# Inversions' transfers on GpSimd's queue, tokens of the first sixteen units listed within the recurrence, those of the last eight counted unit by unit

## The chip, the core and the metric

The kernel runs on one core of one Trainium2 chip. The core has five engines that work side by side, each through its own queue in program order: TensorE (PE, with its weight loads shown as PEld), VectorE (DVE), ScalarE (ACT), GpSimd (POOL) and SyncE (SP), which here only issues transfers. Transfers are issued by SP, ACT or POOL and carried by 16 DMA engines. The metric is the device time of one execution in microseconds (us).

## The reference

An attention-like recurrence over 768 steps (4 batches, 8 heads, head size 40), and behind it a mixture of 8 experts in which each expert keeps only the 80 tokens with the highest gates:

```python
for t in range(S):                       # recurrence, per batch and head
    y[:, :, t] = einsum('bhd,bhde->bhe', r[t], state)
    Sa = einsum('bhde,bhe->bhd', state, a[t])
    state = state * w[t] - outer(Sa, b[t]) + outer(v[t], k[t])
...
x = y as rows, (3072, 320)               # one row per token
logits = x @ w_gate                      # 8 experts
expert_idx = argmax(logits, axis=1)
gate_w = softmax(logits)[expert_idx]
for e in range(8):
    tok_idx = tokens with expert_idx == e
    keep = the 80 of them with the highest gate_w
    out[keep] = gate_w * (relu(x[keep] @ w1[e]) @ w2[e])   # 320 -> 1024 -> 320
```

All other rows of the output are zero.

## The kernel before

The 3072 tokens are cut into 24 units of 128 tokens: 12 chunks of 64 steps times 2 pairs of batches. A unit n goes through `prepare(n)` (decays, scaled keys, the score matrices `nt` and `psi`), waits until the unit triangular matrices of its set are inverted, goes through `solve(n)` (off-diagonal blocks of the inverse) and `finish(n)` (the step of the state: W, UL, the sum into `st`, the decay of `st`, the rows y through `xT` into `xg`, the logits into `lgp`). Units of the same pair depend on each other through `st`, so the 24 finishes are a chain in two strands. Rings of ten buffers (`LOOK = 10`) let prepare run at most ten units ahead of finish, and `nt` has room for three sets.

`invert(j)` inverts the 32x32 blocks of a set of units: sets 0 and 1 have two units, sets 2 to 6 have four (units 4-7, ..., 20-23). Its blocks go to DRAM and come back laid out one block per partition (`out_go`, then `fetch`), 30 elimination steps run on GpSimd (tiles `lt` and `tmp`), the result goes to DRAM (`put`) and comes back into `nt` and `d1` (`back_go` and `low_go`). For sets 2 to 6, `fetch` and `put` are issued by GpSimd, one transfer each of 128 pieces of 4 KB; `out_go` (4 transfers), `back_go` (2) and `low_go` (4) are issued by SP, of 1024, 1024 and 512 pieces of 128 bytes each. `lt` is a single buffer, so a fetch also waits for the put of the set before.

`gate(gi)` turns the logits of four units into gates; every second group (eight units) a ranking of ten rounds (`rank`) on VectorE merges the top 80 of each expert into `cand`.

All this is recorded as operations with engine, estimated cost and dependencies in `Plan`, and `Plan.order()` writes them out as one fixed order per engine: at each step it takes the operation that can start earliest, and among those the one with the lowest `when`, which is half the due time less the length of the chain behind the operation. An engine works through its order strictly; an operation whose input is late holds up all behind it on that engine.

After the last unit a second part runs, engine by engine in plain order: the rest of the ranking, the merge of the eight lists into a threshold per expert (lines 900 to 926), the choice of tokens over all 24 units by comparing gates with the threshold, counting positions and building one-hot matrices (lines 931 to 966), the indices (968 to 974), eight gathers of 80 rows from `x_rows` in DRAM (L991), and then the experts one after the other: transposes of the rows (L1001, L1003), first layer (L1016), second layer (L1035, L1039), output (L1047 to L1051). Expert weights, 2.6 MB each, are loaded by SP as soon as the recurrence's buffers are free (L885, L887).

## Time and profile before

| | us |
|---|---|
| median of 3 runs | 545.68 (545.13 to 548.99) |
| profiled execution, own time | 545.97 |
| its span, first to last instruction | 544.3 |
| outside the span | 1.67 |
| PE / PEld / DVE / ACT / POOL busy | 395.5 / 349.8 / 311.9 / 170.8 / 247.9 |

A row of a timeline is: start, length, engine, line of the program, operation, result <- operands, count; in brackets how long the engine had been idle before it and what ended the idle time. "SPq" and "ACTq" are the queues of transfers, and their lengths are the time that issuing took, not the time to landing. Busy shares are averages over very different stages: up to about 420 us the recurrence runs, from there to 470 us the choice of tokens, and then the experts.

### The profile page before, as it was taken

To read this page: it belongs to the slowest core of one execution; us is meant where nothing else is said; L and a number is where in the kernel's file an instruction comes from. 1 tells how busy PE (TensorE), PEld (TensorE's weight loads), DVE (VectorE), ACT (ScalarE), POOL (GpSimd) and SP (SyncE) were. 2 spreads that over 40 slices of the span, in tenths; PEclk is the share of its full clock that TensorE was granted. 3 is DMA by queue.
4 is the path that set the end of the run, shared out by engine and by line. 5 is a ranking of instruction groups with operands and counts; after the bars stand their busy time and mean duration, and the time that the engine had idled before them with its cause. 6 is when DMAs were issued, how large, how long until landed. Compare 5 with 4: busy or idle time off the path is not lost. (4 is left out here: it accounts for less than half of the span.)

```text
span 544.3 us, 25618 instructions
## 1 busy us (share of the span) xinstructions
PE 395.5 (73%) x11383; PEld 349.8 (64%) x11383; DVE 311.9 (57%) x643; ACT 170.8 (31%) x339; POOL 247.9 (46%) x459
## 2 busy tenths in 40 slices
PE   1834577889958998888888696988795005478995
PEld 1734466778847887777777585878684004377895
DVE  6849956675636675873688543667434785012111
ACT  1521252435523634444534242434251000011100
POOL 7000883699569838982689405882000000501012
PEclk9975797789979997999999589899799555599999
DMA  9668577656595577578766345446400799994000
GB/s 118 99 129 143 85 125 122 128 83 96 118 167 113 95 164 99 107 156 144 122 125 135 88 75 127 95 95 112 88 16 4 218 336 352 297 337 127 17 19 24
DMA packets 233922, 69.39 MB, mean 127 GB/s; under 512 B 214100, under 2 KB 228692, under 8 KB 233812
## 3 DMA queue, kind: packets, MB, share of 16 engines
q1 hardware_dynamic: 200948, 55.76, 50.1%
q10 hardware_dynamic: 30656, 5.12, 5.9%
q0 software_dynamic: 2208, 6.89, 3.9%
q8 instruction: 89, 1.46, 1.1%
q14 instruction: 21, 0.17, 0.1%
HBM read 52.74 MB, written 14.99 MB: 124 GB/s over the span
## 5 line engine op out<-in xcount | busy, mean ns | idle before, releaser
L558 POOL TENSOR_TENSOR tmp<-lt 128x30 f32<-128x30 f32 (+9 forms) x150 | 86.6, 577 | 30.9 <-DMA lt<-blocks 19.5
L560 POOL TENSOR_TENSOR lt<-lt,tmp 128x30 f32<-128x30 f32 (+9 forms) x150 | 89.8, 599 | 11.8
L740 DVE TENSOR_TENSOR UL<-ps,mask 128x832 f32<-128x832 f32 x24 | 24.5, 1022 | 53.7 <-PE ps L735 35.1
L480 PE MATMUL ps<-ah,kbT 40*64 40x64 f32 x1536 | 33.3, 231 | 14.9 <-ACT kbT L471 6.3
L394 PE MATMUL ps<-ident,kb 128*128 128x128 f32 x192 | 33.7, 331 | 10.6 <-ACT lgp L793 4.8
L480 PEld LDWEIGHTS ps<-ah,kbT 40*64 40x64 f32 x1536 | 28.7, 143 | 18.9 <-ACT kbT L471 7.6
L424 DVE TENSOR_TENSOR_SCAN P<-dec,begins 128x520 f32<-128x520 f32 x24 | 31.8, 1324 | 12.4 <-ACT dec L415 12.1
L471 ACT COPY kbT<-ps 128x1024 f32<-128x1024 f32 x24 | 24.3, 1013 | 38.4 <-PE ps L394 30.5
L394 PEld LDWEIGHTS ps<-ident,kb 128*128 128x128 f32 x192 | 27.0, 171 | 14.4 <-ACT lgp L793 5.4
L1051 POOL DMA_INDIRECT out_dram<-y,idx_s x8 | 7.3, 918 | 60.9 <-DVE y L1050 60.9
L1022 DVE TENSOR_SCALAR hT<-hp 128x320 f32<-128x320 f32 x8 | 3.9, 492 | 50.2 <-ACT hT L1024 50.2
L432 DVE TENSOR_TENSOR_SCAN iv<-dec,ends 128x512 f32<-128x512 f32 x24 | 30.5, 1271 | 1.8
L765 DVE TENSOR_TENSOR st<-ps,st 128x832 f32<-128x832 f32 (+1 forms) x24 | 23.9, 994 | 10.0 <-PE ps L754 9.6
L455 DVE TENSOR_TENSOR kb<-rawkb,ps 128x320 f32<-128x320 f32 x48 | 22.4, 479 | 12.4 <-ACT st L711 3.1
L394 PE MATMUL ps<-ident,rawa 128*128 128x128 f32 x96 | 16.7, 302 | 16.9 <-DMA rawa<-in_a_dram 16.9
L1016 PE MATMUL hp<-xe,w 128*64 128x80 f32 x512 | 28.1, 239 | 1.2 <-DVE xe L1005 1.2
L651 ACT COPY rv<-ps 128x1024 f32<-128x1024 f32 x24 | 24.3, 1014 | 12.8 <-PE ps L394 11.2
L695 PE MATMUL ps<-VL,psi 64*64 64x104 f32 x768 | 25.5, 269 | 3.3 <-issue 3.1
L603 DVE STREAM_TRANSPOSE d<-nt 128x256 f32<-128x256 f32 x24 | 10.2, 431 | 30.5 <-DMA nt<-solved 15.9
L735 PE MATMUL ps<-W,nt 64*64 64x104 f32 x768 | 25.5, 273 | 3.1 <-ACT nt L629 1.3
L833 POOL TENSOR_TENSOR ids<-gsm,tok 128x32 f32<-128x32 f32 x6 | 3.2, 531 | 51.4 <-DVE gsm L825 51.3
L415 ACT COPY dec<-ps 128x512 f32<-128x512 f32 x24 | 14.1, 588 | 39.1 <-PE ps L394 30.8
(173 smaller groups left out, 997.1 us busy)
## 6 DMA issues: line engine op xcount, KB each, us to landing
w<-in_moe_w_dram SPq DMA_DIRECT2D x8, 1280.0 KB
w<-in_moe_w_dram SPq DMA_DIRECT2D x8, 1024.0 KB
x_rows<-xg SPq DMA_DIRECT2D x24, 160.5 KB
rawkb<-in_k_dram SPq DMA_DIRECT2D x48, 80.0 KB
rawkb<-in_b_dram SPq DMA_DIRECT2D x48, 80.0 KB
raww<-in_w_dram SPq DMA_DIRECT2D x48, 80.0 KB
rawr<-in_r_dram ACTq DMA_DIRECT2D x96, 40.0 KB
VL<-in_v_dram SPq DMA_DIRECT2D x96, 40.0 KB
```

The lines of the kernel that those rows point to most:

```text
L394: nc.tensor.matmul(o, lhsT=i, rhs=ident, is_transpose=True, **mat)
L424: nc.vector.tensor_tensor_scan(at("P", n), at("dec", n)[:, 0 : H * SEG], begins, 0.0, op0=Alu.mult, op1=Alu.add)
L432: nc.vector.tensor_tensor_scan(at("iv", n)[:, ::-1], at("dec2", n)[:, ::-1], at("ends", n)[:, ::-1], 0.0, op0=Alu.mult, op1=Alu.add)
L471: nc.scalar.copy(at("kbT", n).rearrange("p (k c) -> p k c", k=2), ps[:, bank(kk) : bank(kk) + 2, :])
L480: nc.tensor.matmul(ps[half(to(q, bb)), b0 + q, T * i : T * i + T], lhsT=at("kbT", n)[half(q, D), s0 : s0 + T], rhs=chain(at("ah", n), half ...
L558: e.tensor_tensor(out=tv, in0=m3[:, 0:k_, s : s + 1].to_broadcast([128, k_, n_]), in1=row(s)[:, s + 1 :].unsqueeze(1).to_broadcast([128, k ...
L560: e.tensor_tensor(out=m3[:, 0:k_, s + 1 :], in0=m3[:, 0:k_, s + 1 :], in1=tv, op=Alu.add)
L651: nc.scalar.copy(at("rv", n).rearrange("p (k c) -> p k c", k=2), ps[:, bank(kr) : bank(kr) + 2, :])
L695: nc.tensor.matmul(ps[half(q ^ bb), b0 + q, X * i : X * i + X], lhsT=at("psi", n)[half(bb), 256 * q + T * i : 256 * q + T * i + T], rhs=at ...
L735: nc.tensor.matmul(ps[half(bb), b0 + q, X * i : X * i + X], lhsT=nt[half(x), q, i, :], rhs=at("W", n)[half(x), o : o + X], **mat)
L740: nc.vector.tensor_tensor(out=view(at("UL", n), 0, (M4 * X, 2), (1, M4 * X)), in0=view(ps[:, bank(ku), :], 0, (512, 2), (1, M4 * X)), in1= ...
L1016: nc.tensor.matmul(o[64 * g : 64 * g + 64], lhsT=w[:, 128 * f + 64 * g : 128 * f + 64 * g + 64], rhs=xe[:, c + j * (c == 2), :], start=c = ...
```

## The change

Four things are changed together.

1. For sets 3 to 6 `out_go` is issued by GpSimd, behind the end of the inversion before (the key `("fin", j - 1)`); for sets 2 to 6 `back_go` and `low_go` are issued by GpSimd too.
2. Units 0 to 15 (`NA = 16`): once their gates are known, `choose()` does the merge, the threshold, the choice, the indices (`idx_g`) and eight gathers as operations of the plan, among the work of units 16 to 23. Gates are also split into three bf16 pieces (`parts_`) so that the chosen gates can be picked by bf16 products with the same one-hot matrices. What each chosen token's rank among the 80 is, is worked out as well (`rk_a`).
3. Units 16 to 23 (`NC = 8`) are gated in smaller groups (four, two, one, one), and `count(n)` counts for each token of unit n how many of units 16 to n have the same expert and a higher gate, and adds to the earlier units' counts. `last_count()` then places the tokens of units 16 to 23 among the 80 of units 0 to 15, and a second round of eight gathers overwrites the rows that lose their place. The choice over all 24 units after the recurrence is gone.
4. Smaller moves: for units 20 to 23 the mask of `VL` is done by an ACT copy and a GpSimd product in place of one VectorE product; for units 20 to 22 the product into `xT` goes to GpSimd; `rawr` of units 20 to 23 is loaded by SP. The weights of experts 0 to 6 have buffers, expert 7 takes those of expert 0. A transfer of one element of expert 0's rows stands in SP's queue after the loads of expert 0, so the later weights are issued only when these rows have landed.

```diff
+    NA = 2 * GU * (NM // GU // 3)
+    NC = NM - NA
+    groups = [list(range(n, n + GU)) for n in range(0, NM - GU, GU)] + [[NM - 4, NM - 3], [NM - 2], [NM - 1]]
...
+            by_pool = {"out": 2 < j and not last, "fetch": 1 < j and not last, "put": 1 < j, "back": 1 < j and not late}
+
+            def move(what, n_, lag, fn, reads, writes, after=0.0, to=()):
+                on = by_pool[what]
+                add("POOL" if on else "SP", (0.6 if on else 0.75) * n_, lag, z, fn, reads, writes, None, to, after if on else 0.0)
...
-            add("SP", 3.8, 2.6, z, out_go, [("nt", n) for n in ns], [("blk", j)])
+            move("out", 4, 2.6, out_go, [*(("nt", n) for n in ns), ("fin", j - 1 if by_pool["out"] else -1)], [("blk", j)])
...
-                    nc.sync.dma_start(nt[T * x : T * x + C, :, 0:C], solved[j][x, 0].rearrange("q h (s t) -> s (q h) t", s=C))
-            add("SP", 1.9, 3.0, z + 5, back_go, [("sol", j)], [("nt", n) for n in ns])
+                    queue("back").dma_start(nt[T * x : T * x + C, :, 0:C], solved[j][x, 0].rearrange("q h (s t) -> s (q h) t", s=C))
+            move("back", 2, 3.0, back_go, [("sol", j)], [("nt", n) for n in ns], BACK)
...
-            add("DVE", 0.7, 0.2, z - 1, lv_mask, [klv, ("consts", 0)], [("VL", n)])
+            if n < NM - GU:
+                add("DVE", 0.7, 0.2, z - 1, lv_mask, [klv, ("consts", 0)], [("VL", n)])
+            else:
+                add("ACT", 0.62, 0.2, z - 1, lv_copy, [klv], [("VL", n)])
+                add("POOL", 1.2, 0.2, z - 0.9, lv_keep, [("consts", 0)], [("VL", n)])
...
+        def choose():
+            for i in range(rounds):
+                put("DVE", 1.1 if i < rounds - 1 else 0.5, 0.1, z, best_go, [kM], [kM, kT])
+            put("DVE", 0.7, 0.1, z, sel_go, [kT, *[("gates", g) for g in range(NA // GU)]], [kS])
...
+            for e in range(E):
+                put("POOL", 1.2, 2.5, z + e * 0.01, lambda e=e: nc.gpsimd.indirect_dma_start(
+                    out=rows[e], out_offset=None, in_=x_dram[0][:, :],
+                    in_offset=bass.IndirectOffsetOnAxis(ap=idx_g[:, e : e + 1], axis=0)), [("idx", 0), ("xd", False)], [("row", e)], None, over_rows[e])
...
+            put("POOL", 1.4, 0.1, z, lambda: g_.tensor_tensor(out=gt_, in0=gt_, in1=eq_, op=Alu.add), [kEQ], [kGT])
+            def rank_go():
+                v_.tensor_reduce(rk_a, gt_, axis=AX, op=Alu.add)
+                v_.tensor_scalar_add(rk_a, rk_a, 0.5)
...
+        def count(n, oh):
+            put("DVE", 0.2 + 0.06 * k_, 0.1, z, lambda: v_.tensor_scalar(less[:, 0:nb], o_b[:, 0:nb], gw, None, op0=Alu.is_lt),
+                [("bb", j) for j in range(nb // 128)] + [("gw", g_)], [kLT])
+            put("DVE", 0.35 + 0.13 * k_, 0.1, z, lambda: v_.tensor_tensor_reduce(
+                out=more[:, 0:nk], in0=less[:, 0:nk], in1=all_s(), scale=1.0, scalar=0.0, op0=Alu.mult, op1=Alu.add, accum_out=lt_c[:, kc]),
+                [ks_, kLT], [kMO, ("ltc", k_)])
...
+        def last_count():
+            put("DVE", 0.75, 0.1, z, idx_go, [kid], [("idx", 1)])
+            put("POOL", 8.0, 2.5, z, rows_c, [("idx", 1), ("xd", True)], [("row", e) for e in range(E)])
...
-        for i, op in enumerate((Alu.is_gt, Alu.is_equal)):
-            nc.vector.tensor_tensor(out=sel[:, :, i, :], in0=gates.rearrange("p m e -> p e m"),
-                                    in1=tb.to_broadcast([128, E, NM]), op=op)
...
+        if e == 0:
+            nc.sync.dma_start(sink[:, 0:1], rows[0][0:1, 0:1])
...
+        if e == 1:
+            load_expert(E - 1, *weights[0])
```

How the written order moves, at three places. GpSimd, between the inversion of units 16 to 19 and that of units 20 to 23, before (`solved<-lt` is the put, `lt<-blocks` the fetch):

```order
L577 DMA solved<-lt_138 128x1024
L833 TENSOR_TENSOR ids<-gsm_154,tok 128x32
L536 DMA lt_138<-blocks 128x1024
L558 TENSOR_TENSOR tmp<-lt_138 128x30
L560 TENSOR_TENSOR lt_138<-lt_138,tmp 128x30
```

The same place on GpSimd now (L563 is `out_go` of the next set, L620 `back_go` and L627 `low_go` of the set just inverted, L569 the fetch; L973, L974, L1002 and L1003 fill constants of the counting):

```order
L610 DMA solved<-lt_136 128x1024
L893 TENSOR_TENSOR ids<-gsm_152,tok 128x4x8 x3
L563 DMA blocks<-nt_155 32x32x32 x4
L973 MEMSET rawkb_86 128x128
L974 AFFINE_SELECT rawkb_86<-rawkb_86 128x128
L620 DMA nt_154<-solved 32x32x32 x2
L569 DMA lt_136<-blocks 128x1024
L1002 MEMSET psi_123 128x256
L1003 MEMSET psi_123 128x8
L627 DMA d_0_156<-solved 32x16x32 x4
```

Ten transfers have come between the put and the next inversion's first step, and `back_go` stands behind `out_go` of the next set.

SP, at the same place, before:

```order
L377 DMA VL_131<-in_v_dram 64x4x40 x4
L530 DMA blocks<-nt_157 32x32x32 x4
L587 DMA nt_156<-solved 32x32x32 x2
L594 DMA d_0_158<-solved 32x16x32 x4
L871 DMA out_dram<-zero 384x1x320
L377 DMA VL_132<-in_v_dram 64x4x40 x4
```

SP there now:

```order
L387 DMA rawkb_86<-in_b_dram 64x8x40 x2
L390 DMA VL_129<-in_v_dram 64x4x40 x4
L1252 DMA out_dram<-zero 1536x1x80
L390 DMA VL_130<-in_v_dram 64x4x40 x4
L390 DMA VL_128<-in_v_dram 64x4x40 x4
```

The ten transfers of the inversion have left SP's queue; the loads of inputs follow each other.

VectorE, from the mask of UL of unit 22 to that of unit 23, before:

```order
L740 TENSOR_TENSOR UL_133<-ps,mask 128x832
L671 TENSOR_TENSOR VL_132<-ps,mask 128x2x4x64
L765 TENSOR_TENSOR st_0_144<-ps,st_0_144 128x4x2x64
L775 TENSOR_TENSOR xT_146<-st_0_144,P_92 128x512
L740 TENSOR_TENSOR UL_133<-ps,mask 128x832
```

Now 36 instructions stand between these two masks; the last of them, the mask of unit 23 (L783) and what follows it up to the sum into `st` (L808) (L1167 and L1175 are products with a running sum, of two instructions each):

```order
L1167 ISA dec_79,counts<-ends_133,ps 128x640
L1167 ISA counts 128x1
L1158 SCALAR_TENSOR_TENSOR rawkb_86<-ps,gw_c,rawkb_86 128x128
L1175 ISA rawkb_86,counts<-rawkb_86,ps 128x128
L1175 ISA counts 128x1
L1178 SCALAR_TENSOR_TENSOR counts<-counts 128x1
L783 TENSOR_TENSOR UL_131<-ps,mask 128x832
L1182 TENSOR_TENSOR counts<-counts,ps 128x4
L1161 TENSOR_SCALAR ends_133<-kbT_134,gw_c 128x768
L1158 SCALAR_TENSOR_TENSOR rawkb_86<-ps,gw_c,rawkb_86 128x128
L808 TENSOR_TENSOR st_0_143<-ps,st_0_143 128x4x2x64
```

Counting of units 20 to 22 and the choice over units 0 to 15 stand ahead of the state's own instructions.

## Rows read from the trace of the kernel before

**Rows 1.** Windows by stage: length, busy time of each engine (instructions), granted clock, DMA share, GB/s.
```profile
300.00:350.00 50.00, 40.19 (x1252) 36.25 (x1252) 23.20 (x63) 17.16 (x34) 22.95 (x48) 0.76 0.46 94
350.00:400.00 50.00, 41.79 (x1509) 37.98 (x1513) 31.14 (x74) 18.82 (x37) 18.75 (x34) 0.93 0.46 90
400.00:421.00 21.00, 15.37 (x639) 13.22 (x628) 8.12 (x12) 7.36 (x17) 0.00 (x0) 0.97 0.04 8
421.00:470.00 49.00, 9.63 (x62) 8.11 (x63) 30.44 (x99) 0.23 (x1) 6.15 (x10) 0.50 0.96 299
434.00:462.00 28.00, 9.16 (x60) 7.90 (x60) 19.06 (x51) 0.00 (x0) 0.00 (x0) 0.50 1.06 347
470.00:537.00 67.00, 59.33 (x1444) 55.86 (x1446) 11.14 (x23) 7.16 (x23) 8.50 (x10) 0.97 0.44 129
```

**Rows 2.** Timeline from the last unit's rows to the first expert's transposes.
```profile
418.55 0.69 DVE L775 TENSOR_TENSOR xT<-st,P 128x512 f32<-128x512 f32 x1
...
420.59 0.21 ACT L793 COPY lgp<-ps 128x64 f32<-128x64 f32 x1
...
421.48 0.19 DVE L818 TENSOR_REDUCE gsm<-lg 128x4 f32<-128x32 f32 x1
...
433.72 0.35 DVE L857 MATCH_REPLACE8 cand<-cand,cand 64x208 f32<-64x208 f32 x1
...
463.22 1.02 POOL L991 DMA_INDIRECT rows<-x_rows,idx_g  x1 [0.52 <-DMA w<-in_moe_w_dram]
...
469.94 0.50 PE L1001 MATMUL xp<-ident,rows 80*128 80x80 f32 x2 [8.51 <-DMA rows<-x_rows,idx_g]
```

**Rows 3.** Timeline of GpSimd: puts, fetches and a first step of inversions.
```profile
142.57 0.61 POOL L577 DMA_DIRECT2D solved<-lt  x1 [0.31 <-DMA rawr<-in_r_dram]
148.35 0.54 POOL L536 DMA_DIRECT2D lt<-blocks  x1 [5.17 <-DMA solved<-lt]
...
247.71 0.59 POOL L577 DMA_DIRECT2D solved<-lt  x1 [0.30 <-POOL lt L549]
258.79 0.58 POOL L536 DMA_DIRECT2D lt<-blocks  x1 [10.23 <-DMA rawkb<-in_k_dram]
...
306.63 0.59 POOL L577 DMA_DIRECT2D solved<-lt  x1 [0.30 <-POOL lt L549]
326.74 0.58 POOL L536 DMA_DIRECT2D lt<-blocks  x1 [19.25 <-DMA nt<-solved]
331.41 0.23 POOL L558 TENSOR_TENSOR tmp<-lt 128x30 f32<-128x30 f32 x1 [4.09 <-DMA lt<-blocks]
...
369.54 0.59 POOL L577 DMA_DIRECT2D solved<-lt  x1 [0.30 <-POOL lt L549]
```

**Rows 4.** Timeline of SP's queue: the inversions' transfers around these puts.
```profile
266.46 1.55 SPq L587 DMA_DIRECT2D nt<-solved  x2
...
318.63 4.52 SPq L530 DMA_DIRECT2D blocks<-nt  x4
323.25 1.58 SPq L587 DMA_DIRECT2D nt<-solved  x2
...
377.26 1.16 SPq L587 DMA_DIRECT2D nt<-solved  x2
```

**Rows 5.** Source line of `out_go`: issue times, ns least/median/most, first and last start.
```profile
L530 SPq DMA_DIRECT2D blocks<-nt x28: 302/569/2438, 25.1 to 320.7; - x28
```

**Rows 6.** Source line of the puts (L577): issue to landing, all five.
```profile
DMA to landing us min/median/max: 3.0/3.9/5.5
```

**Rows 7.** Timeline of VectorE: masks of UL in the last units.
```profile
390.66 1.02 DVE L740 TENSOR_TENSOR UL<-ps,mask 128x832 f32<-128x832 f32 x1 [1.07 <-PE ps L735]
...
408.33 1.02 DVE L740 TENSOR_TENSOR UL<-ps,mask 128x832 f32<-128x832 f32 x1 [4.68 <-PE ps L735]
...
415.91 1.02 DVE L740 TENSOR_TENSOR UL<-ps,mask 128x832 f32<-128x832 f32 x1 [4.32 <-PE ps L735]
```

**Rows 8.** Groups by line and form on GpSimd: busy us, mean ns | idle before.
```profile
L558 POOL TENSOR_TENSOR tmp<-lt 128x240 f32<-128x240 f32 x10 | 8.7, 869 | 0.8
```

More of the change, by code (lines that the diff above doesn't have):

```diff
@@ L131 @@
 SLACK = 0.15
+MARGIN = 0.0
+BACK = 20.0
 USE_TAIL = True
+AFTER, CHOICE = 20.0, 10.0
 ALPHA = 0.5
+LATE_R = 4
 LOAD_R, LOAD_V = "ACT", "SP"
@@ L561, in invert @@
                 us = 2 * (0.16 + k_ * n_ / 960) if eng == "DVE" else 2 * (0.185 + 0.00195 * k_ * n_)
-                add(eng, us, 0.1, z + s * 0.1, step, own, [own[-1], tk])
+                add(eng, us, 0.1, z + s * 0.1, step, own, [own[-1], *tks])
             def end():
@@ L572, in end @@
                 diagonal(1.0)
-            add("POOL", 1.45, 0.1, z + 4, end, (), own[-1:])
+            add("POOL", 1.45, 0.1, z + 4, end, (), [own[-1], ("fin", j)])
             def put():
                 if not apart:
-                    nc.gpsimd.dma_start(solved[j].rearrange("x c q h (s t) -> (x c q h) s t", t=C), m3)
+                    queue("put").dma_start(solved[j].rearrange("x c q h (s t) -> (x c q h) s t", t=C), m3)
                     return
@@ L580, in put @@
                 for r in range(2):
-                    nc.sync.dma_start(by[r], m3[half(r)])
-            add("SP" if apart else "POOL", 1.3 if apart else 1.0, 2.8 if apart else 4.0, z + 4.2, put, own[-1:], [("sol", j)])
+                    queue("put").dma_start(by[r], m3[half(r)])
+            move("put", 2 if apart else 1, 2.8 if apart else 4.0, put, own[-1:], [("sol", j)])
             def back_go():
@@ L858, in gate, with left, put @@
                 add("DVE", 0.82 if gs else 0.65, 0.1, z + 2 + 0.3 * i, rank, [("cd", gs)], [("cd", gs), ("cd", gs + 1)])
+        def left(name, m, o, n_, rows_=128, dtype=F32):
+            t = at(name, m)[0:rows_, o : o + n_]
+            return (t if dtype is F32 else t.bitcast(dtype)), ("left", name, m, o)
+        def put(eng, us, lag, when, fn, reads=(), writes=(), psum=None, to=()):
+            add(eng, us, lag, when, fn, reads, writes, psum, [k_[1:3] for k_ in [*reads, *writes] if k_[0] == "left"] + list(to), soft[0])
@@ new lines @@
+        o_b, kO = left("kbT", NM, 0, NC * 128)
+        ohf = [left("raww", NM + i, 0, 512, E) for i in range(2)]
+        ohb, kB = left("rawa", NM, 0, NC * 64, E, BF16)
+        rv_, kRV = left("rawa", NM + 1, 0, 2 * cap, E)
+        gwb = [left("rawa", NM + 1, 160 + 128 * i, 128) for i in range(2)]
+        pick, kPK = left("iv", NM, 0, NC * cap // 2, 128, BF16)
+        hot_c, kHC = left("dec2", NM, 0, NC * cap // 2, 128, BF16)
+        less, kLT = left("ends", NM, 0, 64 * NC, 128, BF16)
+        more, kMO = left("dec", NM, 0, 64 * NC, 128, BF16)
@@ L1055 @@
     ctx.enter_context(tc.manual_schedule())
-    for e in range(E):
-        gather(e)
     turn_x(0)
```

631 lines of the change are left out of this document (419 added, 212 removed).

## The prediction

> **What bounds the kernel now.** Read first the table by stage [rows 1]. Up to 421 us the recurrence runs with PE busy four fifths of the time and no engine full; from 421 to 470 PE is busy for 9.6 of 49 us at a granted clock of 0.50 and nothing else does matrix work; from 470 on the experts run, PE busy 59.3 of 67. The second view is the timeline across that gap [rows 2]: the last unit's product into `xT` ends at 418.55 + 0.69 = 419.24, the ranking of the last eight units at 434.1, then come the merge, the choice and the indices, the first gather is issued at 463.22, and expert 0's rows reach PE at 469.94. So 50.7 us lie between the last unit and the experts, one step waiting for the other. From there to the end of the span are 544.3 - 469.94 = 74.4 us, and 1.67 lie outside it: 419.24 + 50.7 + 74.4 + 1.67 = 545.97, the profiled execution's own time; the median, 545.68, is within 0.3 of it.
>
> The third view is the recurrence's own pace. From a put to the next set's fetch GpSimd took 5.8, 11.1 and 20.1 us (148.35 - 142.57, 258.79 - 247.71, 326.74 - 306.63) [rows 3], and a fetch is followed by the first step 4.7 us later (331.41 - 326.74). The return of the inverted blocks, `back_go`, was issued by SP 18.8, 16.6 and 7.7 us after the put (266.46, 323.25 and 377.26 against 247.71, 306.63 and 369.54) [rows 3, 4], though a put lands within 3.0 to 5.5 us [rows 6]. Inversions and the units that wait for them set the pace.
>
> **The change part by part.** *The choice leaves the gap.* What must follow the last `xT` now, in GpSimd's and VectorE's written order: three comparisons of 320 columns and a running-sum product of 768 columns stand ahead of the logits. With 0.69 us for 512 columns [rows 2] and 1.02 for 832 [rows 7] that is 1.5 + 1.0; the logits themselves are there after 420.59 + 0.21 - 419.24 = 1.6 [rows 2]. Some ten small operations of the gate at 0.19 [rows 2] and a 0.02 gap each give 2.1, so 4.6 so far. Then VectorE's sum for the ranks waits for GpSimd: six gathers at about 1.2 (1.02 and a gap) [rows 2] begin some 6.6 before the end of `xT`, and behind them two products of 640 columns, 2.3 each from 0.87 for 240 [rows 8]: -6.6 + 7.2 + 4.6 = 5.2, and with the sum itself 6.4. From there the counting of units 22 and 23 is VectorE's alone: two comparisons of 896 columns (1.8), products of 896 and 1024 (1.2 and 1.35, with the second instruction that each has), eight picks (1.6), one-hots (0.9) and a dozen small ones (2.6) make 9.5; PE's products 0.5; four index operations 0.8; the first gather 1.1 with its wait; landing 3.0, the least of the puts [rows 6], since the later weights wait behind it. The sum is 21.3, I take 21.5 for 50.7: **-29.2**. No trace shows the running-sum product or the comparison: below, they could take half (4 less), above, half again with a landing of 6.7 as in 463.22 to 469.94 (6 more).
>
> *What the moved work costs where it goes.* The choice took 19.1 us of VectorE within 434 to 462 [rows 1]; for 16 units and with the ranks it is about 20, the counting of eight units some 15, and 9 of ranking go. VectorE has room: busy 23.2 and 31.1 of 50 us, then 8.1 of 21 [rows 1]. The room is not where the orders put it, though. Between the masks of units 20 and 22 I add up 17.7 of VectorE's work against 408.33 - 390.66 = 17.7 now [rows 7], so it fits only without a wait; I add 2. Between those of units 22 and 23 stand 36 instructions: the sum into `st` 0.7, position sums 2.4, two one-hots 1.6, two running-sum products 1.7, the gate of unit 22 1.7, the small ones 3.9, with the mask 13.0 against 415.91 - 408.33 = 7.6 [rows 7], so 5.3 more. Behind the mask of unit 23 come 1.2 more before its `xT`. That is **+8.5** on 28.6 (419.24 - 390.66); bounds 0 (waits for PE now idle VectorE as long [rows 7]) and +14 (each of the two strands also waits for the GpSimd products that replace VectorE's). ACT's added copies are hidden: it is busy 18.8 of 50 and 7.4 of 21 [rows 1]; without that cover five passes per unit at 0.21 [rows 2] and more would cost 1 to 3. The loads of `rawr` that SP takes over and the finer writes of zeros cost nothing as long as SP, without four transfers that took it 4.5 us [rows 4] and six more per set, keeps ahead; if it doesn't, a unit waits some 3 for its `rawr`.
>
> *The inversions' transfers.* SP loses ten transfers per set, GpSimd gains them: four behind the put, two before the fetch, four before the first step. The nearest rows: the same 1024-piece transfers on SP's queue take 0.57 in the median [rows 5], GpSimd's own of 128 pieces 0.54 to 0.61 [rows 3]. They agree, so I take 0.6 to 0.8; below, 0.3 (SP's least); above, 4.6 (0.58 times 1024/128), if GpSimd pays by the piece. At 0.8 a put is followed by the first step after 0.6 + 3.2 + 1.6 + 0.6 + 4.7 = 10.7 (the last four are covered by the fetch's landing), against 5.8 + 4.7 = 10.5 where nothing else held it: no loss there. The return is issued about 6 after its put: 13 earlier than now for units 12 to 15, 10 earlier for 16 to 19. What that brings runs through a loop: unit 23's preparation needs unit 13's finish (`LOOK`), so the last `out_go` (318.63 [rows 4]) and its inversion come earlier by what unit 13 does. The return of the last set stays some 11 after its put, for a `VL` product of unit 20 stands ahead of it. I put unit 20's mask at 380 for 390.66: **-10.7**. Bounds: 0, since `back_go` stands behind `out_go` on GpSimd and waits with it wherever `nt` is late; and -20, if both long gaps shrink to the short one (5.3 and 14.3).
>
> *Experts.* Weights 1 to 7 now load while PE computes, at the rate of the gap (347 GB/s, 2.6 MB in 7.6 us [rows 1]), about PE's own pace; the cover of weights loaded ahead is gone. **+1.0** for PE's stalls under load; bounds 0 and +6.
>
> The sum: 545.97 - 29.2 - 10.7 + 8.5 + 1.0 = 515.6 us, 5.5% less.
>
> [...]
>
> **The rivals.** *Slower: GpSimd pays by the piece.* If one 1024-piece transfer takes c, put to first step is 0.6 + 6c + 0.6 + the larger of 4.7 and 2c. Against today's 10.5, a like one, 15.8 and 24.8 [rows 3], c = 2.3 gives 19.7 and so 9 + 9 + 4 - 5 for the four inversions that have one before them, and 4c - 6 = 3 for the last return, 20 in place of -10.7: 546, no gain left. That is the point from which it decides, four times the rows' 0.58. At 4.6 it is 38 each time, 90 more, with 12 for the last return 102, near 629. For it: the pieces are eight times those of any GpSimd transfer in the trace. Against: the same pieces cost SP no more than others.
>
> *The return stays behind `out_go`.* The change moves the transfers and nothing comes earlier, because GpSimd waits for `nt` exactly where SP did: 323.25 was issued right behind 318.63 [rows 4]. Then 526.3.
>
> *VectorE becomes the bound of the last units.* Recurrence gain 0 and the upper end of the second term, +14: 531.8. For it: the added rows stand ahead of the state's own; against: 4.3 to 4.7 us of idle time before the last masks [rows 7].
>
> *The loop gives all it can.* -20 and +3 for VectorE: 500.8.
>
> **How the numbers follow.** Forecast, 508 to 522: 0.50; return behind `out_go`: 0.15; VectorE bound: 0.15; all of the loop: 0.10; by the piece: 0.10. The range runs from 498, a little below the best case, to 537, above VectorE's case with c up to about 2; it leaves out nearly all of the slower case and some of the edges, 0.18. A measurement of this kernel tells about 1% from no change. All cases but the slower one lie more than 1% below; of that one a small part falls within 1%: faster 0.87, same 0.03, slower 0.10.
>
> **What would show it.** In the changed kernel's trace: the time from the last `xT` to expert 0's transposes near 21 (right) or above 27; GpSimd's 1024-piece transfers under 1 us each, or over 2; `back_go` issued some 6 us after its put, or later with `out_go` ahead of it; unit 20's mask near 380; some 13 us between the last two masks with VectorE busy; the experts' stretch near 75. It is wrong if these transfers are dear, if a written order makes a strand of units wait for a count, or if the weights of expert 0 come late because SP's queue holds them back.

## The result and the profile after

The changed kernel takes 551.54 us in the median of 15 executions (547.74 to 556.27), the kernel before 544.52 beside it: the ratio is 1.0139 (95% interval 1.0108 to 1.017), 1.4% slower where 5.5% faster was forecast. Ratios here leave out executions that lie more than 1.5% above the fastest of their kernel, so they differ from a quotient of the medians, and in the two series of six executions below they rest on three and on two. The profiled execution took 547.74 us, the shortest of the fifteen, with a span of 545.9, so 1.84 lie outside it.

The windows by stage of the changed kernel (columns as in [rows 1]), from the mask of UL of unit 20 to the end of the last `xT`, from there to expert 0's transposes, and from there to the end:

```profile
387.00:434.70 47.70, 37.92 (x1051) 30.48 (x1051) 32.09 (x104) 21.25 (x71) 14.18 (x20) 0.83 0.19 46
434.70:456.10 21.40, 10.85 (x83) 7.66 (x81) 14.65 (x58) 7.14 (x24) 7.83 (x12) 0.50 0.59 191
456.10:545.90 89.80, 68.19 (x1472) 62.91 (x1472) 11.77 (x24) 7.49 (x24) 13.07 (x14) 0.90 0.68 207
```

The gap of 50.7 us is indeed 21.4 now. What it gave was taken back on both sides: the stretch from unit 20's mask to the last `xT` is 47.7 for 28.6, and the experts take 89.75 for 74.4 although TensorE does the same 1472 matmuls there. Set against the forecast's terms:

| term | forecast | measured | missed by |
|---|---|---|---|
| gap, last `xT` to expert 0's transposes | -29.2 | 21.4 - 50.7 = -29.3 | 0 |
| unit 20's mask (390.66 before) | -10.7 | 387.00: -3.7 | +7.0 |
| unit 20's mask to the last `xT` | +8.5 | 47.7 - 28.6 = +19.1 | +10.6 |
| experts' stretch | +1.0 | 89.75 - 74.4 = +15.4 | +14.4 |
| sum, from 545.97 | 515.6 | 547.7 (0.2 more outside the span) | +32 |

These are single executions. In nine profiled executions with all of the inversions' transfers on GpSimd's queue (this one and those of the experiments) unit 20's mask stands at 387.0 to 399.4, at 390.0 in the median, so the -3.7 of this row is the favourable end of that spread: the gain of the second term is nearer to nothing.

The timeline of the gap, changed kernel, for comparison with [rows 2]:

```profile
434.03 0.68 DVE L818 TENSOR_TENSOR xT<-st,P 128x512 f32<-128x512 f32 x1
...
438.73 0.80 DVE L1113 TENSOR_REDUCE small_a<-kb 80x8 f32<-80x640 f32 x1
...
453.06 0.16 DVE L1218 SCALAR_TENSOR_TENSOR idx_c<-small_a 80x8 int32<-80x8 f32 x1
...
453.49 1.00 POOL L1223 DMA_INDIRECT nt<-x_rows,idx_c  x1 [11.94 <-DVE small_a L1231]
...
456.15 0.50 PE L1295 MATMUL xp<-ident,nt 80*128 80x80 f32 x2 [3.59 <-DMA nt<-x_rows,idx_c]
```

The ranks' sum ends 4.8 us after `xT`, the indices are there at 453.2, and expert 0's rows reach TensorE 2.7 us after the first gather's issue began: the parts differ from the forecast's by a few us (6.4; 9.5 of counting, here 12.3), the sum does not.

GpSimd's transfers, to be read beside [rows 3, 5]. The source line of `out_go` in the changed kernel (ns least, median, most) with the time from the start of an issue to its landing, in us:

```profile
L563 POOL DMA_DIRECT2D blocks<-nt x16: 783/784/840, 145.6 to 320.6; - x16
DMA to landing us min/median/max: 4.8/5.4/6.0
```

GpSimd's timeline of the changed kernel around two puts (L610 the put, L563 `out_go`, L620 `back_go`, L569 the fetch):

```profile
144.95 0.61 POOL L610 DMA_DIRECT2D solved<-lt  x1 [0.31 <-POOL lt L582]
145.56 3.17 POOL L563 DMA_DIRECT2D blocks<-nt  x4
148.72 1.56 POOL L620 DMA_DIRECT2D nt<-solved  x2
154.21 0.57 POOL L569 DMA_DIRECT2D lt<-blocks  x1 [3.93 <-DMA x_rows<-xg]
...
259.63 0.61 POOL L610 DMA_DIRECT2D solved<-lt  x1 [0.30 <-POOL lt L582]
260.24 3.13 POOL L563 DMA_DIRECT2D blocks<-nt  x4
263.38 1.24 POOL L893 TENSOR_TENSOR ids<-gsm,tok 128x32 bf16<-128x32 f32 x3
265.56 1.58 POOL L620 DMA_DIRECT2D nt<-solved  x2 [0.94 <-DMA solved<-lt]
268.87 0.58 POOL L569 DMA_DIRECT2D lt<-blocks  x1 [1.73 <-DMA blocks<-nt]
```

A transfer of 1024 pieces takes GpSimd 0.78 us in the median of 16, 0.84 at most, one of 128 pieces 0.57 to 0.61 in these rows: it does not pay by the piece. `back_go` is issued 3.8 and 5.9 us after these puts (about 6 was forecast). But from put to fetch it now takes 9.3, 10.1, 9.2 and 9.6 us, where before it took 5.8, 5.4 (199.89 - 194.50), 11.1 and 20.1 (148.35 - 142.57 and so on, [rows 3]): the long waits shrank, the short ones grew. The last put is at 369.84, before at 369.54.

VectorE's masks of UL of units 20, 22 and 23 in the changed kernel's timeline, for [rows 7]:

```profile
387.00 1.02 DVE L783 TENSOR_TENSOR UL<-ps,mask 128x832 f32<-128x832 f32 x1 [0.68 <-PE ps L778]
...
409.70 1.02 DVE L783 TENSOR_TENSOR UL<-ps,mask 128x832 f32<-128x832 f32 x1 [0.93 <-ACT sT L729]
430.68 1.02 DVE L783 TENSOR_TENSOR UL<-ps,mask 128x832 f32<-128x832 f32 x1 [5.45 <-remote]
```

TensorE's timeline ahead of the last of these masks (L749, L762 and L778 are unit 23's steps towards it, L797 its product of keys with VL; rows of the choice and the counting in between):

```profile
416.26 0.68 PE L830 MATMUL ps<-wsel,xT 40*64 40x48 f32 x32 [1.18 <-ACT raww L1142]
417.60 0.69 PE L749 MATMUL ps<-rv,sT 40*64 40x64 f32 x32 [0.65 <-ACT xg L841]
...
420.53 1.67 PE L762 MATMUL ps<-st,ah 40*64 40x104 f32 x32
422.13 0.71 PE L1155 MATMUL ps<-rawa 8*128 8x512 bf16 x2
422.77 0.47 PE L1148 MATMUL ps<-ident,rawa 128*128 128x128 f32 x1
...
423.39 1.67 PE L778 MATMUL ps<-W,nt 64*64 64x104 f32 x32
424.83 0.69 PE L797 MATMUL ps<-VL,kb 64*64 64x64 f32 x12
426.31 0.47 PE L797 MATMUL ps<-VL,kb 64*64 64x64 f32 x2 [0.79 <-issue]
...
429.17 0.48 PE L797 MATMUL ps<-VL,kb 64*64 64x64 f32 x4 [0.95 <-issue]
430.58 0.54 PE L797 MATMUL ps<-VL,kb 64*64 64x64 f32 x9 [0.93 <-issue]
```

From mask 22 to mask 23 it is 21.0 us, not 13. Three things are seen. TensorE's row of unit 23's steps (L749, L762, L778) is broken by the choice's and the counting's (L1155, L1148, and between 418.2 and 420.5 the 32 picking products), and it waits 1.18 us ahead of L830, put down to ACT's copy of the counting (L1142), before the recurrence goes on. L762 takes 1.67 where it took 0.94 at a granted clock of 1.00 (at 406.28): the clock is 0.66 in the mean of 415 to 425 and 0.50 in 425 to 435, after a stretch in which PE was busy 3.2 of 5 us (415 to 420); before, it was 0.97 up to 421 [rows 1]. And L797, 32 matmuls that took 0.64 us at a granted clock of 1.00 (at 409.38), takes from 424.83 to 431.1 with gaps put down to "issue", that is, the engine waited for nothing that the profile shows. Six gathers of the first round (L1086) are issued from 422.0 to 429.1.

The windows from mask 20 to mask 22 and from there to mask 23 (columns as in [rows 1]):

```profile
387.00:409.70 22.70, 18.90 (x627) 15.76 (x630) 17.51 (x58) 13.29 (x43) 5.30 (x9) 1.00 0.26 58
409.70:430.68 20.98, 15.42 (x389) 12.01 (x381) 11.03 (x39) 7.96 (x28) 8.88 (x11) 0.70 0.16 40
```

VectorE has about the work that was counted for it, 17.5 and 11.0 us (forecast 17.7 and 13.0), and stands idle for 15.1 us of the 43.7. TensorE is the fuller engine in both.

### The profile page after: what moved, and what is told of

The parts are those of the page before. It is cut to its first block, busy times and chain, and to the rows that moved or that the text cites. A ratio compares the mean times of both kernels' runs of the same rounds, so it can differ in the third digit from the quotient of the medians.

```text
span 545.9 us, 25994 instructions
## 1 busy us (share of the span) xinstructions
PE 422.3 (77%) x11456; PEld 368.1 (67%) x11456; DVE 325.3 (60%) x718; ACT 188.6 (35%) x411; POOL 308.5 (57%) x552
## 3 DMA queue, kind: packets, MB, share of 16 engines
q8 instruction: 90, 1.47, 1.1%
## 5 line engine op out<-in xcount | busy, mean ns | idle before, releaser
L593 POOL TENSOR_TENSOR lt<-lt,tmp 128x30 f32<-128x30 f32 (+9 forms) x150 | 92.2, 615 | 11.8
L591 POOL TENSOR_TENSOR tmp<-lt 128x30 f32<-128x30 f32 (+9 forms) x150 | 84.8, 565 | 21.7 <-DMA lt<-blocks 10.3
L783 DVE TENSOR_TENSOR UL<-ps,mask 128x832 f32<-128x832 f32 x24 | 24.5, 1022 | 40.0 <-PE ps L778 23.5
L493 PE MATMUL ps<-ah,kbT 40*64 40x64 f32 x1536 | 36.2, 238 | 12.6 <-ACT kbT L484 7.8
L1310 PE MATMUL hp<-xe,w 128*64 128x80 f32 x512 | 31.9, 250 | 8.9 <-issue 7.8
L1310 PEld LDWEIGHTS hp<-xe,w 128*64 128x64 f32 x512 | 27.3, 151 | 10.4 <-issue 8.8
L407 PE MATMUL ps<-ident,kb 128*128 128x128 f32 x192 | 28.8, 298 | 5.1 <-DVE xT L591 3.1
L658 PE MATMUL ps<-d,gt 64*64 64x32 f32 x768 | 22.2, 238 | 9.8 <-DMA d<-solved 7.9
L808 DVE TENSOR_TENSOR st<-ps,st 128x832 f32<-128x832 f32 (+1 forms) x24 | 23.8, 990 | 9.9 <-PE ps L797 9.7
L644 PE MATMUL ps<-d,nt 64*64 64x32 f32 x768 | 19.8, 238 | 12.1 <-DVE d L636 5.6
L797 PE MATMUL ps<-VL,kb 64*64 64x104 f32 (+1 forms) x768 | 25.8, 264 | 4.2 <-issue 4.0
L778 PE MATMUL ps<-W,nt 64*64 64x104 f32 x768 | 27.5, 283 | 1.8 <-issue 1.8
L407 PE MATMUL ps<-ident,rawa 128*128 128x128 f32 x96 | 19.0, 330 | 12.6 <-DMA rawa<-in_a_dram 12.6
L407 PEld LDWEIGHTS ps<-ident,kb 128*128 128x128 f32 x192 | 23.5, 153 | 7.6 <-POOL ah L593 3.2
```

The source lines that it names most:

```text
L407: nc.tensor.matmul(o, lhsT=i, rhs=ident, is_transpose=True, **mat)
L493: nc.tensor.matmul(ps[half(to(q, bb)), b0 + q, T * i : T * i + T], lhsT=at("kbT", n)[half(q, D), s0 : s0 + T], rhs=chain(at("ah", n), half ...
L591: e.tensor_tensor(out=tv, in0=m3[:, 0:k_, s : s + 1].to_broadcast([128, k_, n_]), in1=row(s)[:, s + 1 :].unsqueeze(1).to_broadcast([128, k ...
L593: e.tensor_tensor(out=m3[:, 0:k_, s + 1 :], in0=m3[:, 0:k_, s + 1 :], in1=tv, op=Alu.add)
L778: nc.tensor.matmul(ps[half(bb), b0 + q, X * i : X * i + X], lhsT=nt[half(x), q, i, :], rhs=at("W", n)[half(x), o : o + X], **mat)
L783: nc.vector.tensor_tensor(out=view(at("UL", n), 0, (M4 * X, 2), (1, M4 * X)), in0=view(ps[:, bank(ku), :], 0, (512, 2), (1, M4 * X)), in1= ...
```

## The experiments

Theory A, formed from these rows: three separate losses, none of which is the transfers' issue time. The fetch waits behind `out_go`; the choice and the counting stand in the way of the last units; and the experts, whose weights now load while they run, get their instructions late beside that traffic. What A and B mean in a run stands in its expectation. Times are medians; the ratio is to the kernel before, executed beside each.

**The choice ranked last.**

```diff
-AFTER, CHOICE = 20.0, 10.0
+AFTER, CHOICE = 1000.0, 1000.0
```

> The changed kernel with every step of the choice and of the counting ranked behind all of the recurrence (two weights of the written order raised from 20 and 10 to 1000). Theory A, the listing and counting inside the recurrence lengthen its end: the last xT, at 434.7 in the changed kernel, comes at 418 to 425, and the gap to expert 0's transposes grows from 21.4 to 45 to 55. Theory B, the recurrence's end is late for the transfers on GpSimd's queue: the last xT stays within 4 us of 434.7. Either way the experts' stretch of 89.8 stays above 85 if the weights behind the sink set it (they still wait for expert 0's rows), and falls to about 75 if it is the short gap alone that leaves them late.

548.83 us, ratio 1.0145 (1.0058 to 1.0231). Neither theory was put to the test: the planner looks first at which operation can start earliest, the rank only breaks ties, and the choice stayed about where it was (masks 389.71, 400.17, 410.90, 435.86). The tokens picked are not all the reference's in this order, most likely because some one-hots are read after the next gate has overwritten them; the work is as much.

**The inversions' transfers on SP's queue.**

```diff
-            by_pool = {"out": 2 < j and not last, "fetch": 1 < j and not last, "put": 1 < j, "back": 1 < j and not late}
+            by_pool = {"out": False, "fetch": 1 < j, "put": 1 < j, "back": False}
```

> The changed kernel with the inversions' out_go, back_go and low_go on SP's queue again, as before the change; the choice stays as changed. Theory A, this part nets to nothing (784 ns apiece on GpSimd's queue, fetches 4 us later in short gaps and earlier in long ones): unit 20's UL mask within 5 us of 387, the total within 5 us of the changed kernel. Theory B, GpSimd's queue is what makes the recurrence end at 434.7: the last xT is 8 us or more earlier and the total 8 us or more shorter. My first forecast, that this part gains 10.7 us, would make this kernel that much slower, some 562.

540.46 us (528.92 to 547.15) against 540.7 before: too scattered for a ratio, so it was done again:

> The run with the transfers on SP's queue once more, with more rounds. Theory A, GpSimd's queue holds the next fetch behind out_go where the gap from put to fetch is short: fetches 3 to 4 us after the puts of the sets of units 4 to 7 and 8 to 11 (9.3 and 10.1 in the changed kernel), the last put near 362.5, unit 20's mask at 379 to 383, and the total 7 to 12 under the changed kernel, within 1% of the kernel before. Theory B, the first run was a lucky one: unit 20's mask near 387 and a total near 550.

539.08 us against 544.76, ratio 0.9862 (0.9766 to 0.9958): 1% below the kernel before by the medians, 2.3% below the changed one. GpSimd's timeline at the first put in the first of the two:

```profile
143.01 0.62 POOL L610 DMA_DIRECT2D solved<-lt  x1 [0.31 <-DMA rawkb<-in_k_dram]
146.76 0.54 POOL L569 DMA_DIRECT2D lt<-blocks  x1 [3.13 <-DMA solved<-lt]
```

SP had issued `out_go` at 124.10, well ahead of the put, so the fetch waits for the put's landing alone: 3.75 and 3.25 us in the two short gaps (9.3 and 10.1 in the changed kernel), 10.3 and 12.1 in the long ones. In the two runs the last put is at 362.50 and 363.51, 6 to 7 us earlier, and unit 20's mask at 380.40 and 385.57. In the nine profiled executions with all transfers on GpSimd's queue that mask stands at 387.0 to 399.4, six of them below 392; in the three with SP's it stands at 380.4, 385.6 and 386.7. By the medians, 390.0 and 385.6, this part costs some 4 us at unit 20, within a spread of single executions that is larger. That the part nets to nothing, as theory A of the first run had it, does not hold there, and theory A of the second holds in direction, though 385.57 lies outside its 379 to 383. The totals say less than they seem to: of the 13.0 and 8.0 us by which these two spans are shorter than the changed kernel's, 7.5 and 7.9 lie in the experts' stretch (82.3 and 81.8 for 89.75), which comes back below.

**`out_go` alone on SP's queue.**

```diff
+            by_pool = {"out": False, "fetch": 1 < j, "put": 1 < j, "back": 1 < j}
```

> The changed kernel with out_go alone on SP's queue again; back_go and low_go stay on GpSimd's. Theory A, what costs in this part of the change is out_go's place behind the inversion before: the gaps from put to fetch of the two short cases are 3 to 5 us as with all transfers on SP's queue, the last put stands at 361 to 366, unit 20's mask at 378 to 385, total 534 to 543. Theory B, back_go and low_go on GpSimd's queue cost as much (they stand ahead of the next fetch there): the gaps stay above 7 us and the total above 545.

543.47 us against 544.54, ratio 0.987 (0.98 to 0.9941; 0.998 by the medians). The gaps are 5.6, 10.6, 14.2 and 14.3 us, the last put is at 374.73 and unit 20's mask at 389.87: all but the first gap speak for theory B. The total lies between the two, 0.5 above A's and 1.5 below B's. The rows after the third put tell why:

```profile
252.74 0.62 POOL L610 DMA_DIRECT2D solved<-lt  x1 [0.30 <-POOL lt L582]
253.37 0.63 POOL L893 TENSOR_TENSOR ids<-gsm,tok 128x32 bf16<-128x32 f32 x3
256.28 1.62 POOL L620 DMA_DIRECT2D nt<-solved  x2 [2.28 <-ACT rv L684]
264.33 2.58 POOL L627 DMA_DIRECT2D d<-solved  x4 [6.42 <-PE ps L658]
266.89 0.58 POOL L569 DMA_DIRECT2D lt<-blocks  x1
```

`low_go` waits 6.4 us for PE to be done with its buffer, and the fetch stands behind it. In this row it is not `out_go`'s place that costs but that of another transfer with a wait of its own between a put and the next fetch on one queue. The time lies below the changed kernel's all the same; how much of that is this part stays open, as the profiled execution does not show it.

**The choice and the counting behind the recurrence**, by letting the planner take their steps only when no other step is open, and keeping each gate's buffer until its readers are done:

```diff
-                key = (max(t, free + SLACK), o["when"], i)
+                key = (max(t, free + SLACK) + HOLD * o["soft"], o["when"], i)
...
+HOLD = 1000.0
```

> The changed kernel, where the planner takes a step of the choice or of the counting only when no other step is open (the run with raised ranks had not moved them). Theory A, these steps inside the recurrence lengthen its end: last xT at 414 to 423 instead of 434.7, and a gap of 45 to 58 instead of 21.4. Theory B, the end is late for another reason: last xT stays within 4 us of 434.7. The stretch behind it stays above 82 either way, since the later weights still wait for expert 0's rows.

Two executions, 570.49 and 740.07 us, so no ratio; the first is the profiled one, with a span of 568.8. VectorE's masks of units 20 and 23 in its timeline:

```profile
392.15 1.02 DVE L784 TENSOR_TENSOR UL<-ps,mask 128x832 f32<-128x832 f32 x1 [2.26 <-PE ps L779]
...
420.10 1.02 DVE L784 TENSOR_TENSOR UL<-ps,mask 128x832 f32<-128x832 f32 x1 [3.35 <-PE ps L779]
```

28.0 us between them, against 43.7 in the changed kernel and 25.3 before [rows 7]. So 15.7 of the 18.4 us by which these four units became longer go when the choice, the counting and the first gathers leave them (L797's breaks with them; the granted clock is 0.94 over the 28 us). The last `xT` itself came only at 431.6, since this order puts unit 23's product behind others', outside the forecast 414 to 423; the gap was 51.7 (45 to 58 forecast).

**The first round of gathers behind the last `xT`**, moved in the list of operations from the choice to the last counting, with one more condition:

```diff
-                    in_offset=bass.IndirectOffsetOnAxis(ap=idx_g[:, e : e + 1], axis=0)), [("idx", 0), ("xd", False)], [("row", e)], None, over_rows[e])
+                    in_offset=bass.IndirectOffsetOnAxis(ap=idx_g[:, e : e + 1], axis=0)), [("idx", 0), ("xd", False), ("xT", NM - 1)], [("row", e)], None, over_rows[e])
```

> The changed kernel with the eight gathers of the first round of rows (units 0 to 15) made to wait for the last xT, behind the recurrence. Theory A, the 5 us without any engine at work before unit 23's UL mask are an instruction block of TensorE's that comes late beside those gathers: the broken-up matmuls of L797 close up, units 20 to 23 take 37 to 40 us in place of 43.7, and the total falls by 3 to 6. Theory B, the block is late without them: units 20 to 23 stay at 42 to 45.

542.44 us, ratio 0.9991 (0.9947 to 1.0035): 1.5% less than the changed kernel, more than theory A's 3 to 6 us. TensorE ahead of unit 23's mask:

```profile
427.63 1.67 PE L778 MATMUL ps<-W,nt 64*64 64x104 f32 x32
429.07 1.32 PE L797 MATMUL ps<-VL,kb 64*64 64x64 f32 x32
```

The broken matmuls of L797 have closed up, at the same half clock, and units 20 to 23 take 39.35 us, as A has it. One gather of the eight still goes ahead of the last `xT`, at 426.25. But the gathers are not shown to be the cause. Two runs below, those that read two experts' weights in turn, leave the recurrence and its gathers as they are, and the same matmuls are whole in them as well. The first of the two, with gathers issued at 431.11, 432.43 and 433.67:

```profile
433.93 1.32 PE L797 MATMUL ps<-VL,kb 64*64 64x64 f32 x32
```

Units 20 to 23 take 41.0 and 40.8 us in these two, 43.7 to 46.8 in the four executions with the breaks (the changed kernel, and the runs with traffic alone, with half the instructions and without the transfer that holds the weights back), though the first gather is issued 2.8 us ahead of L797 in all six. Nor does a late packet of instructions show: the queue that is read below as TensorE's moves nothing between 420.8 and 432.8 in the changed kernel, while L797 goes on by one to twelve matmuls at a time and is done by 431.1. What breaks these matmuls in some executions stays open.

The rest, 8 us, came where it was not looked for: the experts' stretch is 81.6 in place of 89.75, 3.8 less in expert 0's first layer (6.8 from its transposes to the last of hT, instead of 10.6) and the rest in the later experts. Of the other runs with all the loads, four have 81.6 to 82.4, three 83.2 to 85.5, and one has 90.0.

**Weights: the traffic, or the wait for them?** First with the weights of experts 0 and 1 in turn, in both layers:

```diff
-        (w1, w1r, _), xe = weights[e], xes.pop(e)
+        (w1, w1r, _), xe = weights[e % 2], xes.pop(e)
...
```

> All eight experts' weights are loaded as in the changed kernel, but TensorE multiplies with those of experts 0 and 1 alone (the outputs of experts 2 to 7 are so left wrong), so that no matmul waits for a later load while the traffic stays. Theory A, the experts' stretch of 89.8 us is long since TensorE's instructions come late under the traffic of the weights: the stretch stays at 85 to 91, with idle time put down to issue inside the layers, total 543 to 552. Theory B, TensorE waits for late weights: the stretch falls to 76 or less, total about 537.

570.26 us, ratio 1.0449 (1.0337 to 1.0561): expert 2 reads the tile into which expert 7's weights are loaded, and TensorE waits 36.5 us for that load, so the run does not tell the two theories apart. With `weights[min(e, 1)]` in both layers:

> All weights are loaded as in the changed kernel, but TensorE multiplies with expert 0's for expert 0 and with expert 1's for all the others (outputs of experts 2 to 7 left wrong): the traffic stays, no matmul waits for a load after expert 1's. It replaces the run that alternated between experts 0 and 1, where expert 2 then waited for expert 7's load into expert 0's tile. Theory A, TensorE's instructions come late under the weights' traffic (16 KB blocks every 7 to 8 us while it lasts, every 4 to 5 after it): experts' stretch 85 to 91, with idle time put down to issue. Theory B, the layers wait for late weights: stretch 76 or less.

551.66 us, ratio 1.0129 (1.0082 to 1.0175), and a stretch of 549.8 - 459.83 = 90.0 us: no layer after expert 1 depends on a load, and nothing is won. Theory A. Then the first two experts' weights in turn, without the other loads at all:

```diff
-    for e in range(E - 1):
+    for e in range(2):
...
-            load_expert(E - 1, *weights[0])
+            pass
```

> As the run that reads experts 0's and 1's weights alone, and the other six are not loaded at all (outputs of experts 2 to 7 left wrong): traffic and dependence both gone from about 462. Both theories: the experts' stretch falls to 70 to 76 and the total to 532 to 537. If neither the traffic nor the late weights make the stretch long (a low clock after the wait, say), it stays above 85.

529.85 us, ratio 0.9784 (0.9682 to 0.9887), stretch 525.5 - 454.2 = 71.3. So of the 90 us some 18.5 are the traffic. Where they lie shows in the windows of the whole stretch: with traffic alone, with two experts' weights, and with late gathers, to be read beside 456.10:545.90 above.

```profile
459.80:549.80 90.00, 71.34 (x1472) 66.49 (x1472) 11.78 (x24) 7.47 (x24) 13.11 (x14) 0.84 0.67 207
454.20:525.50 71.30, 61.24 (x1472) 57.99 (x1472) 11.68 (x24) 7.45 (x24) 12.98 (x14) 0.95 0.14 40
456.20:537.80 81.60, 63.30 (x1472) 59.31 (x1472) 11.68 (x24) 7.48 (x24) 12.01 (x13) 0.94 0.72 226
```

Two things add up. TensorE's idle time put down to "issue" is 11.8 us in the changed kernel, 8.8 with traffic alone, 8.5 with late gathers and nothing without traffic. And the same 1472 matmuls keep TensorE busy for 68.2, 71.3, 63.3 and 61.2 us, since the granted clock is lower: 0.90, 0.84, 0.94 and 0.95. So of the changed kernel's 18.5 us 11.8 are waits and 7.0 the clock, and the run with late gathers is 8.2 us shorter by 3.3 of waits and 4.9 of clock. In the changed kernel the clock is 0.50 from 490.0 to 493.3 and from 513.9 to 520.6, each time at the end of or behind one of the longest of these waits (3.51 us up to 490.27, 2.73 up to 513.14), and 1.00 from 493.5 to 513.8.

How the waits come about shows in equal windows of 46 us. The changed kernel under traffic, from the windows:

```profile
468.00:514.00 46.00, 34.31 (x818) 32.26 (x820) 5.29 (x11) 3.70 (x12) 2.80 (x3) 0.96 1.05 321
```

The instruction queue q8 in the same window, from the view of transfers (packets, MB, share):

```profile
q8 instruction: 6, 0.10, 0.9%
```

The run with traffic alone, windows:

```profile
472.00:518.00 46.00, 36.75 (x821) 34.76 (x823) 5.79 (x12) 3.69 (x12) 2.80 (x3) 0.91 1.04 320
```

The run with two experts' weights, windows, and below it the same queue:

```profile
466.00:512.00 46.00, 43.74 (x1126) 41.82 (x1122) 8.17 (x17) 5.55 (x18) 4.62 (x5) 1.00 0.05 14
```

```profile
q8 instruction: 9, 0.15, 1.4%
```

TensorE does 820 matmuls and as many weight loads in one, 1125 in the other: about 270 and 250 instructions to a packet of 16 KB. The queue moves 90 packets in the whole span (1.47 MB), 255 to each for TensorE's 22,912 instructions; by these counts it is read as TensorE's, the view does not name the engine. In the changed kernel they move at 472.4, 479.8, 487.7, 495.5, 503.0 and 510.5, every 7 to 8 us, and at 514.8, 522.1, 527.4, 531.8 and 537.6 when the weights are in; in the run without traffic every 5.6 us in the mean. That pace by itself only mirrors TensorE's. What ties the waits to the packets is their place: in that window 6.2 + 3.5 + 0.5 us of idle time are put down to "issue", in five waits, which end at 482.18, 490.27, 498.10, 505.82 and 513.14, each 2.4 to 2.8 us after one of the packets began to move; only the packet at 472.4 has none behind it. The six of the run with late gathers end 2.4 to 2.7 us behind its packets, and without traffic there is none. (Four short waits within expert 0's first layer, 1.6 us together, have no packet ahead of them.) That TensorE's next instructions are late is read from these times; the trace has no row that names them.

**Half the instructions**, 128 columns of weights to a matmul in both layers:

```diff
-                    for g in range(2):
-                        nc.tensor.matmul(o[64 * g : 64 * g + 64], lhsT=w[:, 128 * f + 64 * g : 128 * f + 64 * g + 64],
-                                         rhs=xe[:, c + j * (c == 2), :], start=c == 0, stop=c == 2)
+                    nc.tensor.matmul(o, lhsT=w[:, 128 * f : 128 * f + 128],
+                                     rhs=xe[:, c + j * (c == 2), :], start=c == 0, stop=c == 2)
...
```

> The changed kernel, whose experts' layers take 128 columns of weights in one matmul in place of two with 64 (96 to 48 and 64 to 32 matmuls an expert, and as many weight loads): half the instructions for the same bytes. Theory A, instructions come late under the traffic: the idle time put down to issue goes, and if a 128-column matmul takes no longer than one of 64 the stretch falls from 89.8 to 70 to 80. Theory B, late weights set the stretch: it stays above 84. If a wide matmul takes twice as long, the part after the traffic (7.6 us an expert) stays as it is and only the stalls go.

633.45 us, ratio 1.1551 (1.1385 to 1.1718). The same 46 us of traffic:

```profile
464.00:510.00 46.00, 43.92 (x217) 42.62 (x217) 3.50 (x7) 2.06 (x7) 4.26 (x5) 0.50 1.05 329
```

No wait of TensorE in the stretch is put down to issue, under the same traffic; it is busy for 43.92 of these 46 us, against 34.31 in the changed kernel. But a wide matmul costs far more than two narrow ones (last section), so the gain cannot be read off; this supports theory A only as far as an engine that needs few instructions is not held up.

**Without the transfer that holds the later weights back.**

```diff
-        if e == 0:
...
-            nc.sync.dma_start(sink[:, 0:1], rows[0][0:1, 0:1])
```

> The changed kernel without the transfer behind which the later weights wait for expert 0's rows. Theory A (instructions late under the traffic): the traffic only starts some 5 to 12 us earlier and expert 0's rows land 1 to 4 us later beside it; total within 5 us of the changed kernel. Theory B (late weights set the stretch): the stretch falls by the 5 to 12 us that they come earlier.

549.99 us, ratio 1.0109 (1.0052 to 1.0167): within 2 us of the changed kernel. The rows land later (PE waits 7.1 us for them instead of 3.6), the stretch is 556.7 - 475.07 = 81.6. The total is as theory A has it, the stretch as theory B: it is 8.1 us shorter with weights that start earlier. As the run with late gathers has the same 81.6 with the transfer in place, and the one without dependence on a load has 90.0, the shorter stretch does not need earlier weights; this run alone does not decide it.

**SP's queue and late gathers together.**

> Both at once: the inversions' transfers on SP's queue and the first round of gathers behind the last xT. If each is worth what the runs apart say and they add, unit 20's mask stands near 380 to 382, units 20 to 23 take 37 to 40, the gap 21 to 25 and the stretch 82 to 90: 533 to 541, one per cent under the kernel before at best. If the experts' stretch takes up what comes earlier, it stays at 540 to 545.

541.45 us, ratio 0.9974 (0.993 to 1.0018): the two do not add. Unit 20's mask is at 386.71, units 20 to 23 take 41.9 us, the gap is 24.0, the stretch 82.4.

## Why the prediction was wrong

*The gap* (-29.2) was right to 0.1 us, parts a few us off.

*The inversions' transfers* (-10.7, measured -3.7). The step that failed is "no loss there": put to first step was added up as 0.6 + 3.2 + 1.6 + 0.6 + 4.7, the issue times alone, with the landing counted once, for the fetch. A fetch also waits for its own `out_go` to land, whose issue now comes behind the put: 0.6 + 3.1 us of issue, 5.2 to 6.4 us more to the fetch, and once 0.6 for a step between, which makes the 9.2 to 10.1 of the four gaps. In three of them the wait ahead of the fetch is put down to `out_go`. In the short gaps before, SP had finished issuing `out_go` at 131.75 and 195.35, well ahead of the put at 142.57 and beside that at 194.50. `back_go` did come 4 to 6 us after its put, about as forecast, but the last put stands at 369.84 for 369.54: what it brought through the loop was lost in the gaps. The runs with SP's queue put the price of this part at some 4 us at unit 20, with a larger spread between executions. The rival "GpSimd pays by the piece" falls: 0.78 us in the median of the 16 `out_go` transfers and 0.84 at most, with VectorE busy for 9.5 of the 12.6 us in which they were issued. The rival "the return stays behind `out_go`" named a wait at the right place and the wrong transfer: the fetch, not the return.

*What the moved work costs where it goes* (+8.5, measured +19.1, beyond the upper bound of +14). The step that failed is the count on VectorE alone: its work was counted about right (17.5 and 11.0 us measured for 17.7 and 13.0), but 22.7 and 21.0 us passed, so VectorE's row does not set the pace. TensorE's row is mixed as well, its steps stand behind those of the choice and the counting and behind waits for ACT's copies, and its granted clock is 0.50 in 425 to 435 where it had been 0.97 up to the end of the recurrence. With choice, counting and first gathers behind the recurrence the four units take 28.0. L797's breaks, some 4 us of the 43.7, are a part whose cause stays open: they are gone in the run that moves the gathers, but also in two that do not. Of the text's signs of error the nearest, a written order that makes a strand of units wait for a count, happened on TensorE and ACT.

*Experts* (+1.0, measured +15.4, bounds 0 and +6). The step that failed is "about PE's own pace": the cover that went was named and priced by the wrong resource. The rate of the weights (7.6 us an expert) does match TensorE's pace, and lateness of the weights is not the trouble; the traffic itself is. Beside it experts 3 to 5 take 12.0 us each (the last part of their hT is begun at 479.44 for expert 2 and at 515.46 for expert 5), without it 7.6. Of the 90 us 18.5 are shown to be the traffic: 11.8 of TensorE's waits for nothing that the profile shows and 7.0 of a lower granted clock. That the waits are late instructions is read from the packets ahead of each, and is supported, not proved, by the run with half the instructions. The kernel before had shown such waits: its timeline of TensorE while its last weights were loading has

```profile
489.12 0.36 PE L1016 MATMUL hp<-xe,w1r 128*64 128x80 f32 x4 [1.77 <-issue]
...
496.59 0.28 PE L1039 MATMUL zp<-hT,w 128*64 128x80 f32 x1 [1.58 <-issue]
```

and none behind them, with packets at 486.7 and 494.1. That is 3.4 us in some 27 us of loading, and the change makes the loading beside the experts more than twice as long. Why the same traffic makes the stretch 81.6 in some runs and 90 in others is open in its cause, not in its place: it is the length of the waits and the clock behind them.

## What to carry to other kernels

A wait in which transfers run was worth less here than its length: the gap gave 29.3 us, and the experts' stretch, beside which the weights now load, grew by 15.4. Ask what the traffic under it will do to the work that it will then run beside, not only whether the bytes arrive in time, and look in the trace of before for engines that wait for nothing beside such traffic. When steps are moved into a tight recurrence, count them on every engine whose order they enter, not only on the one with room. And a transfer moved to another queue brings its landing along: whatever reads its result waits from the new place (here the fetch, issued 5.2 to 6.4 us after the issue of `out_go` ended). Two profiled executions of one written order differed here by 5.2 us up to unit 20's mask (380.40 and 385.57, the runs with SP's queue); a difference of that size wants more than one of them.

## What was not expected of the hardware

- Beside 320 GB/s of weights the instruction queue that is read as TensorE's moved a packet of 16 KB every 7 to 8 us, and TensorE did 820 matmuls in 46 us; without, nine packets and 1125 matmuls. Its waits for nothing that the profile shows ("issue") from 468 to 514 us ended 2.4 to 2.8 us after a packet began to move.
- A float32 matmul of 128 x 128 weights on 80 columns took 1.6 times two of 128 x 64: 32 wide ones took 7.06 us at a granted clock of 0.50, 0.22 each; in the changed kernel 64 narrow ones took 4.30 us at a mean of 0.54 (from 516.74), 0.067 each, and 2.43 us at 1.00 (from 526.22). With the wide ones the clock stayed at 0.50 from 480 to 600 us with PE busy 117.66 of 120 us, where the changed kernel had 0.96 from 468 to 514 and 0.87 behind it. Half the instructions cost 82 us more.
- GpSimd issued transfers of 1024 pieces of 128 bytes in 0.78 to 0.84 us each, those of 128 pieces of 4 KB in 0.57 to 0.62 but for one of 0.80; the former landed 4.8 to 6.0 us after the issue began, where the trace shows it.
